# A recurrent attention kernel: one 32-row pass per segment, the left-over rows batched over four segments

## The chip, the cores and the metric

One core of a Trainium2 chip runs the whole kernel. The metric is the device time of one execution in microseconds (us), the median over several runs. A time difference under 2% counts as "the same".

## The reference, cut to what matters

```python
def reference(A_x, A_mem0, A_Wq, A_Wk, A_Wv, A_Wo, A_seg_len, B_x, B_w_r, B_w_gate, B_w_up, B_w_down):
    # x: 1 x 2048 x 1024 bf16; 32 heads of 128; memory M = 8 rows; segments of 32 tokens, so 64 segments
    xn = _layernorm(A_x)
    mem = A_mem0
    for s in range(64):                                  # strictly one after the other, through mem
        h = concat([mem, xn[32*s : 32*s+32]])            # 40 rows
        q, k, v = h @ Wq, h @ Wk, h @ Wv                 # each weight 1024 x 4096
        p = softmax(mask(q @ k.T * scale))               # per head 40 x 40
        o = (p @ v) @ Wo                                 # 4096 x 1024
        mem = o[:8];  outs.append(o[8:])
    # B: the two tokens with the highest router value go through a gated MLP (1024 -> 3584 -> 1024)
    return A_x + concat(outs) + B(xn)
```

The four attention weights are 8 MB each, 32 MB together. Both kernels keep a part of them on chip and stream the rest from HBM (the chip's main memory) again in each of the 64 segments. What comes before the first segment (LayerNorm, the router, the expert MLP of B, the loads of the kept weights) is called the prologue.

## The kernel before

A segment has 40 rows, and the kernel places them on blocks of 32 columns of TensorE's array. So the kernel before makes two passes over every weight: a main pass (PSm: 8 memory rows and 24 token rows) and a left-over pass (PSl: the last 8 token rows, padded to 32). Each group of four matmuls, one per 32-column block of the array, adds one term to a 128x512 result. When a result is complete, ScalarE or VectorE copies it out of TensorE's accumulators; this copy is called its evacuation. The weights are cut into 32 granules (pieces that are loaded as one) of 1 MB; 19 stay on chip and 13 are streamed per segment through four slots (buffers that a granule holds from its issue until TensorE has read it).

```python
N_RES = 19
N_STREAM_BUFS = 4
GCOLS = 4096
# ...
    def get_granule(g):
        if g in res_tiles:
            return granule_view(res_tiles[g], g)
        t = wstream.tile([P, GCOLS], BF16, tag="g")
        nc.sync.dma_start(out=granule_view(t, g), in_=granule_dram(g))
        return granule_view(t, g)
# ...
        for p in range(6):
            mat, half = divmod(p, 2)
            PSm = psA.tile([P, 512], F32, tag="st")
            PSl = psA.tile([P, 512], F32, tag="st")
            for gi in range(KC // 2):
                g = (mat * 2 + half) * (KC // 2) + gi
                Gv = get_granule(g)
                for kk in range(2):
                    kc = 2 * gi + kk
                    for j in range(4):
                        nc.tensor.matmul(PSm[32 * j:32 * j + SEG, :], lhsT=ST[:, kc, :], rhs=Gv[:, kk, 512 * j:512 * (j + 1)],
                                         start=(kc == 0), stop=(kc == KC - 1), tile_position=(0, 32 * j))
                    for j in range(4):
                        nc.tensor.matmul(PSl[32 * j:32 * j + SEG, :], lhsT=STL[:, kc, :], rhs=Gv[:, kk, 512 * j:512 * (j + 1)],
                                         start=(kc == 0), stop=(kc == KC - 1), tile_position=(0, 32 * j))
                for fn in deferred.pop((p, gi), []):
                    fn()
# ... softmax of all heads at once, its tail after the last projection:
            nc.vector.reciprocal(out=DEN[:, 0:NCOL], in_=DEN[:, 0:NCOL])
# ... output projection: two row groups of 32, N = 512
                for dh in range(2):
                    for a in range(2):
                        nc.tensor.matmul(WO[64 * dh + 32 * a:64 * dh + 32 * a + 32, :],
                                         lhsT=OTf[:, NQ * h + 32 * a:NQ * h + 32 * a + 32], rhs=Gv[:, hh, 512 * dh:512 * (dh + 1)],
                                         start=(n_done == 0), stop=(n_done == H - 1), tile_position=(0, 64 * dh + 32 * a))
# ... the small loads and the output stores are issued by GpSimd, the streamed weights by the sync engine:
            nc.gpsimd.dma_start(out=XNR[64 * dh + M:64 * dh + NQ, :], in_=xn_d[t0:t0 + SEG, 512 * dh:512 * (dh + 1)])
```

## Time and profile before

| | before |
|---|---|
| time, median of 4 runs | 3061.8 us (3060.8 to 3063.8) |
| first segment starts at | 210 us |
| one segment | 44.4 us, 64 of them |
| TensorE busy | 82% |
| DMA, mean over the span | 309 GB/s |

These are lines of the page of the kernel before: busy time by engine, and the shares of the chain of work that ended last, by engine and by line.

```profile
...
PE 2510.8 (82%) x44661; PEld 1177.5 (38%) x44725; DVE 1017.0 (33%) x2235; ACT 493.1 (16%) x1013; POOL 344.2 (11%) x782
...
DMA packets 304707, 946.07 MB, mean 309 GB/s; under 512 B 21088, under 2 KB 21104, under 8 KB 304304
...
PE 71%; DVE 17%; DMA 4%; issue 4%; ACT 2%; POOL 1%; another core or an unknown queue 0%; POOLq 0%; DVEq 0%; ACTq 0%
PE PSm L464 20%; PE WO L498 19%; PE PSl L467 18%; PE PTq L377 5%; DVE DEN L425 5%; PE OTP L443 1%; PE OTP L440 1%; DVE MB L169 1%; DVE VM L169 1%; DVE VLs L169 1%; DMA out_dram<-OUTB 1%; ACT MB L169 1%; PE WO L502 1%; DVE NM L395 1%; DVE NMX L405 1%
...
```

The chain says who sets the time: TensorE with 71%, then VectorE (DVE). DMA is only 4% of it. The next lines are the table of time stretches: the whole segment phase, then one segment cut into its stages. The columns are start and end, length, busy time of each engine with its instruction count, the granted TensorE clock, the mean busy share of the 16 DMA engines, and GB/s.

```profile
...
core 0: us, PE busy (x) PEld busy (x) DVE busy (x) ACT busy (x) POOL busy (x), PEclk, DMA share, GB/s
0.00:210.00 210.00, 37.84 (x701) 28.19 (x702) 84.05 (x285) 7.94 (x23) 43.15 (x90) 1.00 0.72 270
210.00:3055.00 2845.00, 2472.98 (x43960) 1149.30 (x44023) 932.92 (x1951) 485.13 (x990) 301.06 (x692) 0.92 0.87 313
1542.79:1568.40 25.61, 25.33 (x469) 11.76 (x470) 9.04 (x22) 4.76 (x11) 1.84 (x4) 1.00 0.97 362
1568.40:1574.68 6.28, 2.89 (x89) 1.75 (x90) 4.36 (x5) 0.59 (x1) 0.26 (x1) 0.84 0.83 312
1574.68:1584.70 10.02, 9.97 (x134) 4.13 (x134) 0.00 (x0) 0.69 (x1) 0.32 (x2) 0.76 0.63 189
1584.70:1587.24 2.54, 0.56 (x8) 0.30 (x5) 1.90 (x6) 0.90 (x2) 2.54 (x6) 1.00 0.88 273
...
```

The third row is the projection stage (25.6 us, TensorE busy for 25.33 of it), then the softmax tail, the output projection at a clock of 0.76, and the handing over of the memory rows. In the projection stage, with a DMA share of 0.97, the weights arrive at 362 GB/s.

### The profile page before, as it was taken

What the parts mean: (1) busy time and instruction counts of PE and PEld (TensorE: products, weight loads), DVE (VectorE), ACT (ScalarE), POOL (GpSimd) and SP (SyncE); (2) the same over time, 40 slices, a digit from 0 to 9 for tenths busy, and PEclk for the clock granted to TensorE, in tenths of its full rate; (3) what the DMA queues carried; (4) which work ended last, traced back from release to release, by engine and by line L of the source; (5) the groups of instructions that cost most, each with busy time, mean ns of one, the idle gap of its engine ahead of it and who ended that gap; (6) DMA issues with size and microseconds to landing.
All of it is one profiled execution on the core that took longest, in us unless ns stands there. A gap on an engine that the chain in (4) does not pass through costs nothing.

```text
span 3059.5 us, 96413 instructions
## 1 busy us (share of the span) xinstructions
PE 2510.8 (82%) x44661; PEld 1177.5 (38%) x44725; DVE 1017.0 (33%) x2235; ACT 493.1 (16%) x1013; POOL 344.2 (11%) x782
## 2 busy tenths in 40 slices
PE   0068888888888888888898888889888888888887
PEld 0043443344444434433443443344344434433443
DVE  5403333332333333333333333333333233333322
ACT  0001111111111111111111111111111111111111
POOL 3201011101101110110011011101101110111010
PEclk9999999999999999999999999999999999999998
DMA  9298898888889888888988898889889888988886
GB/s 378 92 378 302 317 329 303 309 326 308 305 315 330 305 304 319 328 302 308 333 307 299 319 329 303 307 321 321 297 316 333 303 303 315 330 303 309 328 312 220
DMA packets 304707, 946.07 MB, mean 309 GB/s; under 512 B 21088, under 2 KB 21104, under 8 KB 304304
## 3 DMA queue, kind: packets, MB, share of 16 engines
q1 hardware_dynamic: 287904, 914.41, 82.5%
q0 software_dynamic: 16400, 25.49, 2.5%
q8 instruction: 350, 5.73, 0.7%
q14 instruction: 53, 0.43, 0.0%
HBM read 931.42 MB, written 8.40 MB: 307 GB/s over the span
## 4 chain that ended last, share of the span: by engine, by line
PE 71%; DVE 17%; DMA 4%; issue 4%; ACT 2%; POOL 1%; another core or an unknown queue 0%; POOLq 0%; DVEq 0%; ACTq 0%
PE PSm L464 20%; PE WO L498 19%; PE PSl L467 18%; PE PTq L377 5%; DVE DEN L425 5%; PE OTP L443 1%; PE OTP L440 1%; DVE MB L169 1%; DVE VM L169 1%; DVE VLs L169 1%; DMA out_dram<-OUTB 1%; ACT MB L169 1%; PE WO L502 1%; DVE NM L395 1%; DVE NMX L405 1%
## 5 line engine op out<-in xcount | busy, mean ns | idle before, releaser
L464 PE MATMUL PSm<-wres,STn 128*32 128x512 bf16 x7168 | 723.2, 381 | 1.0 <-issue 1.0
L467 PE MATMUL PSl<-wres,STLn 128*32 128x512 bf16 x7168 | 720.0, 379 | 1.3 <-issue 1.3
L464 PE MATMUL PSm<-t,STn 128*32 128x512 bf16 x5120 | 517.1, 382 | 23.9 <-DVE STn L169 13.3
L467 PE MATMUL PSl<-t,STLn 128*32 128x512 bf16 x5120 | 514.1, 379 | 0.0
L464 PEld LDWEIGHTS <-STn 128*32 128x32 bf16 x12288 | 342.0, 96 | 387.7 <-issue 46.7
L467 PEld LDWEIGHTS <-STLn 128*32 128x32 bf16 x12288 | 346.8, 97 | 262.1 <-issue 8.7
L498 PE MATMUL WO<-wres,OTf 128*32 128x512 bf16 x5120 | 399.3, 463 | 0.0
L498 PEld LDWEIGHTS <-OTf 128*32 128x32 bf16 x8192 | 239.5, 114 | 327.5 <-issue 182.9
L440 PE MATMUL OTP<-NMX,VM 32*128 32x40 bf16 x2048 | 96.2, 194 | 198.2 <-DVE NMX L426 144.0
L169 DVE CAST MB<-WO 8x512 bf16<-8x512 f32 x63 | 43.1, 684 | 635.9 <-PE WO L502 330.6
L498 PE MATMUL WO<-t,OTf 128*32 128x512 bf16 x3072 | 252.8, 461 | 0.0
L425 DVE RECIPROCAL DEN<-DEN 128x320 f32<-128x320 f32 x64 | 138.7, 2167 | 170.7 <-PE DEN L424 170.7
L169 DVE CAST XBm<-PSm 128x512 bf16<-128x512 f32 x128 | 88.5, 691 | 307.6 <-PE PSm L464 276.0
L169 DVE CAST XBl<-PSl 128x512 bf16<-128x512 f32 x128 | 88.5, 692 | 232.9 <-PE PSl L467 230.9
L443 PEld LDWEIGHTS <-VLs 32*128 32x128 bf16 x2048 | 78.8, 104 | 205.0 <-issue 205.0
L169 ACT CAST MB<-WO 8x512 bf16<-8x512 f32 x63 | 36.3, 576 | 645.1 <-PE WO L502 328.9
L169 ACT CAST XBm<-PSm 128x512 bf16<-128x512 f32 x128 | 75.0, 586 | 371.5 <-PE PSm L464 349.3
L506 POOL MEMSET MB<- 128x512 bf16 x63 | 33.1, 525 | 851.9 <-PE PTq L377 851.9
L169 ACT CAST XBl<-PSl 128x512 bf16<-128x512 f32 x128 | 75.0, 586 | 292.4 <-PE PSl L467 292.4
L432 POOL MEMSET OTf<- 128x24 bf16 x64 | 7.6, 118 | 876.6 <-PE WO L498 876.1
L377 PE MATMUL PTq<-IDENT,XBm 128*128 128x128 bf16 x1024 | 101.6, 222 | 5.6 <-DVE XBm L169 4.4
L185 PE MATMUL PT<-IDENT,MB 128*128 128x128 bf16 x256 | 24.7, 219 | 97.4 <-ACT STn L169 50.1
(152 smaller groups left out, 2208.9 us busy)
## 6 DMA issues: line engine op xcount, KB each, us to landing
t<-in_A_Wq_dram SPq DMA_DIRECT2D x256, 1024.0 KB, 6.4
t<-in_A_Wk_dram SPq DMA_DIRECT2D x192, 1024.0 KB, 7.7
t<-in_A_Wv_dram SPq DMA_DIRECT2D x192, 1024.0 KB, 8.5
t<-in_A_Wo_dram SPq DMA_DIRECT2D x192, 1024.0 KB, 8.2
Gt<-in_B_w_gate_dram SPq DMA_DIRECT2D x8, 896.0 KB, 12.8
Gt<-in_B_w_up_dram SPq DMA_DIRECT2D x8, 896.0 KB, 8.1
Gt<-in_B_w_down_dram SPq DMA_DIRECT2D x7, 1024.0 KB, 8.0
wres<-in_A_Wk_dram SPq DMA_DIRECT2D x5, 1024.0 KB, 24.4
```

The source lines that it names most:

```text
L169: eng(out=out_ap, in_=in_ap)
L377: nc.tensor.transpose(out=PTq[:, il * P:(il + 1) * P], in_=XBx[:, il * P:(il + 1) * P], identity=IDENT[:, :])
L395: nc.vector.tensor_reduce(out=NM3[:, 0, :], in_=S_main[:, 0:NCOL].rearrange("p (b k) -> p b k", k=32), axis=AX.X, op=ALU.max, apply_transp ...
L405: nc.vector.transpose(out=NMBT, in_=NMX[:, 0:NCOL])
L425: nc.vector.reciprocal(out=DEN[:, 0:NCOL], in_=DEN[:, 0:NCOL])
L440: nc.tensor.matmul(OTP[:, jl, i * NQ:(i + 1) * NQ], lhsT=VM[32 * j:32 * j + SEG, i * P:(i + 1) * P], rhs=P_main[32 * j:32 * j + SEG, i * N ...
L443: nc.tensor.matmul(OTP[:, jl, i * NQ:(i + 1) * NQ], lhsT=VLs[32 * j:32 * j + SEG, i * P:(i + 1) * P], rhs=P_left[32 * j:32 * j + SEG, i * ...
L464: nc.tensor.matmul(PSm[32 * j:32 * j + SEG, :], lhsT=ST[:, kc, :], rhs=Gv[:, kk, 512 * j:512 * (j + 1)], start=(kc == 0), stop=(kc == KC - ...
L467: nc.tensor.matmul(PSl[32 * j:32 * j + SEG, :], lhsT=STL[:, kc, :], rhs=Gv[:, kk, 512 * j:512 * (j + 1)], start=(kc == 0), stop=(kc == KC ...
L498: nc.tensor.matmul(WO[64 * dh + 32 * a:64 * dh + 32 * a + 32, :], lhsT=OTf[:, NQ * h + 32 * a:NQ * h + 32 * a + 32], rhs=Gv[:, hh, 512 * d ...
L502: nc.tensor.matmul(WO[:, :], lhsT=IDENT[:, :], rhs=XR[:, :], start=False, stop=True, skip_group_check=True)
L506: nc.gpsimd.memset(MB[:, :], 0.0)
```

## The change

The intent: take TensorE's work down, and take the stream down with it. The left-over rows of four segments (4 x 8 = 32 rows) make one full pass per four segments; the output projection likewise. The softmax is done by halves of the heads, hidden under projection phases. Half-MB granules let 42 of 64 stay on chip, so 22 x 0.52 = 11.5 MB are streamed per segment in place of 13.6. The price: queries and keys of the left-over rows go through DRAM and come back per segment; the residual, the transposed input rows and the left-over rows' results are further small transfers; and nearly all of them are issued on the weights' own queue.

```diff
-N_RES = 19
-N_STREAM_BUFS = 4
+N_RES = 42
+N_SLOT = 4
+PHASES = [(0, 0), (1, 0), (0, 1), (1, 1), (2, 0), (2, 1)]
... (prologue rewritten: LayerNorm, router and transposes per 128-row tile, results stored to DRAM)
+    def load_st(s):
+        ST = stp.tile([P, KC, SEG], BF16, tag="st", name="ST")
+        nc.sync.dma_start(out=ST.rearrange("p k r -> p (k r)"), in_=xT_d[s // 4][s % 4])
+    def load_stl(g):
+        nc.sync.dma_start(out=STL.rearrange("p k r -> p (k r)"), in_=stl_d[g][:, :])
+    def load_r(s):                       # four loads per segment; load_ql: two loads (QL, KL)
+            nc.sync.dma_start(out=R[32 * g + M:32 * g + SEG, :], in_=xr_d[s * SEG:s * SEG + XM, 256 * g:256 * (g + 1)])
...
+        G, j = divmod(s, 4)
+        if s == 0:
+            left = {0: 0, 1: 0, 2: 0}
+        elif j == 0:
+            left = {2: G}                # V of the left-over rows
+        elif j <= 2 and G + 1 < NT:
+            left = {j - 1: G + 1}        # Q, K of the next four segments' left-over rows
...
+        hook(2, 5, lambda: scores(0))
+        hook(4, 5, lambda: scores(1))
+        hook(5, 2, lambda: attend(0, 0))
+        hook(5, 5, lambda: attend(0, 1))
...
             for kc in range(KC):
+                Gv = granule(8 * p + kc)
+                for jq in range(4):
+                    nc.tensor.matmul(PSm[32 * jq:32 * jq + 32, :], lhsT=ST[:, kc, :], rhs=Gv[:, 512 * jq:512 * (jq + 1)],
+                                     start=(kc == 0), stop=(kc == KC - 1), tile_position=(0, 32 * jq))
+                if PSl is not None:      # only where this segment has a left-over pass
...
         if s + 1 < NSEG:
+            qkl_n = load_ql(s + 1)
+            ST_n = load_st(s + 1)
+            load_r(s + 1)
+            if j == 0 and G + 1 < NT:
+                STL = load_stl(G + 1)
...
+        if j == 3:
+            for g in range(4):
+                for sg in range(4):      # 16 loads of 8 rows
+                    nc.sync.dma_start(out=RL[32 * g + XL * sg:32 * g + XL * (sg + 1), :],
+                                      in_=xr_d[t0:t0 + XL, 256 * g:256 * (g + 1)])
...                                      # and 16 stores of 8 rows from ScalarE's queue (OL)
```

Here j is the segment's place in its group of four. Q and K of the left-over rows of a group are made in the group before it, V and the output in the group itself.

## The prediction

> **What bounds the kernel now.** The table of time stretches, over one segment of 44.45 us (x64 = 2845 us, after a 210 us prologue): 25.6 us of projection passes with TensorE 99% busy; 6.3 us around the softmax tail, where TensorE waits 2.25 us (the reciprocal takes 2.17); 10.0 us of output projection; 2.5 us handing the memory rows to the next segment. So TensorE's chain sets the time (71% of the chain of waits, DMA 4%). In the timeline a group of four 128x512 matmuls advances every 0.216 us; 96 such groups (half for the 8 left-over rows) make 20.7 us, 32 output groups another 6.9. The clock records show 0.5 for 6.8 us in nearly every segment, after the softmax wait; the output groups then take 0.43 us (the Trainium skill, "TensorE: Matmul & The Clock Gate", Part 1, says an idle window halves the clock; the trace agrees). DMA is close behind: 13 one-MB granules per segment; packets of 4096 B take 159 ns and of 2048 B 84 ns on 16 engines (412 and 390 GB/s), so about 33.5 us.
>
> **What changes.** The left-over pass runs once per four segments: 48 + 12 groups, minus 7.8 us. The output projection covers 32 rows, N=256: 3.5 us plus 0.9 on average, minus about 5 us with its half clock. Softmax comes per half, hidden under projections. Hand-over needs one copy, two transposes, one copy: about 1.3 us. I sum TensorE's chain to about 24 us. Streamed weights fall to 22 half-MB granules: 16x1.27 + 6x1.34 = 28.4 us, plus about 1 us of small loads.
>
> **Where the limit goes.** To the weight stream: 29.5 us exceeds 24, so part of TensorE's gain is lost. Nor is the stream continuous. The fastest 1 MB load lands 4.9 us after issue, 2.5 of it data, so fixed latency is about 2.3 us and four half-MB slots (5.1 us of data) leave only about 1 us slack ("DMA: Bandwidth & Descriptors" puts the fixed cost near 2 us). Bubbles I add (estimates): 2 us per segment from hand-over and attention; seven small loads ahead of the output granules at 0.37 us issue each; every fourth segment sixteen 8-row residual loads (about 7 us of queue) that TensorE waits for, then sixteen 8-row stores on ScalarE's queue ahead of the next evacuation (about 6 us). The built program's order shows eight DMA completion semaphores shared by all of these. Estimate: 31.5, 32, 39 and 38 us for the four segments; with half clock in some stalls about 35.5 on average. Prologue: LayerNorm about 4.5 us per tile, expert weights 55 us: about 160 us.
>
> **Predicted: 2430 us** (0.79 of before); 2270 to 2680 eight times in ten. Faster by over 2%: 0.96; within 2%: 0.02; slower: 0.02.
>
> **Right if** DMA is the busiest unit, above 85% in segments at 320 to 340 GB/s; TensorE's matmuls wait mostly for streamed granules; matmuls drop to about 36,000; segments differ with period four, the longest pair around the memory of the fourth; the granted clock stays above 0.8.
>
> **Wrong if** segments are even near 31 us (small transfers free: 2150); or TensorE, about 65% loaded, falls to half clock for most of a segment, when a segment needs 45 us and the gain vanishes; or the attention pieces, now in program order with single buffers, hold TensorE longer than the stream does; or half-size granules stream below 390 GB/s.

## The result, and the profile after

The changed kernel takes 3178.9 us (median of 4 runs, 3167.4 to 3188.6) against 3061.8. The ratio is 1.038, with a 95% interval of 1.0355 to 1.0405: slower, where 0.79 was predicted. (Ratios here are the mean time of one kernel's runs over that of the other's runs of the same rounds, so they are not quite the ratio of the quoted medians.)

| | before | predicted | after |
|---|---|---|---|
| first segment starts at, us | 210 | 160 | 249 |
| mean segment, us | 44.4 | 35.5 | 45.7 |
| segments by j = 0, 1, 2, 3, us | even | 31.5 to 39 | 53.9, 42.0, 41.0, 45.9 |
| matmuls | 44,661 | about 36,000 | 36,305 |
| DMA in the segments | 0.87, 313 GB/s | over 0.85, 320 to 340 | 0.78, 264 |
| granted clock in the segments | 0.92 | above 0.8 (whole run) | 0.82 (whole run 0.836) |

The segments with j = 0 include the very first, which makes three left-over passes; without it their mean is 53.0 us. The two terms of the miss are 249 - 160 = 89 us of prologue and 64 x (45.7 - 35.5) = 653 us of segments.

The page of the changed kernel, the same parts as above (the DMA lines read: packets, MB and mean rate; then packets, MB and share of 16 engines of the weights' queue):

```profile
...
PE 2005.7 (63%) x36305; PEld 1010.8 (32%) x36305; DVE 737.7 (23%) x2158; ACT 447.1 (14%) x1001; POOL 87.9 (3%) x292
...
DMA packets 366682, 831.69 MB, mean 262 GB/s; under 512 B 73428, under 2 KB 118516, under 8 KB 366328
...
q1 hardware_dynamic: 343800, 813.86, 75.8%
...
DMA 57%; PE 25%; DVE 6%; SPq 4%; issue 2%; ACT 2%; ACTq 0%; POOL 0%; DVEq 0%; POOLq 0%
DMA g<-in_A_Wo_dram 16%; DMA g<-in_A_Wq_dram 16%; DMA g<-in_A_Wv_dram 11%; PE PSm L489 10%; DMA g<-in_A_Wk_dram 7%; PE WO L540 6%; PE PSl L493 3%; SPq L532 2%; DMA out_dram<-OB 2%; PE PTq L396 1%; DMA kl_d<-QS 1%; PE WL L540 1%; DMA QL<-ql_d 1%; DVE SPS L438 1%; DVE NM L437 1%
...
```

TensorE's matmuls fell as intended, and its busy time by 505 us (2510.8 to 2005.7). In the segments that is 8.4 us each (38.6 to 30.2, at a granted clock of 0.92 and 0.82), where the prediction's two subtractions, 7.8 and about 5 us, make 12.8. And the chain moved: DMA has 57% of it, TensorE 25%. And yet the busiest DMA queue is at 75.8% only, and all DMA together moves 262 GB/s. So the kernel waits for a stream that isn't running at its rate. The table of stretches of the changed kernel (three of the prologue, the segment phase, and two stretches inside a segment pair):

```profile
...
0.00:144.00 144.00, 35.09 (x384) 26.86 (x384) 60.13 (x245) 35.65 (x49) 38.92 (x36) 1.00 0.62 193
144.00:175.00 31.00, 0.71 (x13) 0.47 (x11) 8.19 (x20) 4.58 (x6) 0.00 (x0) 1.00 0.87 314
175.00:249.00 74.00, 34.18 (x510) 19.79 (x509) 4.32 (x7) 1.03 (x2) 0.00 (x0) 0.94 0.80 276
249.00:3175.00 2926.00, 1935.75 (x35406) 963.65 (x35402) 665.03 (x1887) 405.87 (x945) 48.98 (x256) 0.82 0.78 264
1567.00:1582.20 15.20, 11.41 (x186) 4.76 (x183) 4.68 (x14) 2.37 (x7) 0.38 (x2) 0.78 0.35 125
1582.20:1605.00 22.80, 14.00 (x266) 7.65 (x265) 2.56 (x8) 2.77 (x6) 0.00 (x0) 0.85 0.90 302
...
```

Compare the last two rows. From 1567.0 to 1582.2 us the DMA engines are at 0.35; in the next 22.8 us they are at 0.90 and 302 GB/s. What holds the stream in the first one is seen in the timeline of the sync engine's DMA queue (start, duration of the issue, line, transfer):

```profile
...
1562.90 4.62 SPq L323 DMA_DIRECT2D g<-in_A_Wv_dram  x4
1570.18 0.38 SPq L347 DMA_DIRECT2D QL<-ql_d  x1
1570.61 0.47 SPq L347 DMA_DIRECT2D KL<-kl_d  x1
1571.12 0.47 SPq L328 DMA_DIRECT2D ST<-xT_d  x1
1571.63 1.62 SPq L339 DMA_DIRECT2D RT<-xr_d  x4
1581.76 0.36 SPq L333 DMA_DIRECT2D STL<-stl_d  x1
1582.16 1.97 SPq L323 DMA_DIRECT2D g<-in_A_Wo_dram  x4
```

Between the end of the last Wv granule's issue at 1567.5 and the first Wo granule at 1582.16 no weight is asked for. QL has to wait for its buffer (the queue's own waits, shown below, put 135.5 us over 63 such loads down to the scores that still read it), then KL, ST and four RT follow, and STL waits until 1581.76: its single buffer is being read by the left-over pass of V. All the streamed Wo granules stand behind it in program order, though their four slots are free: four are issued in 1.97 us as soon as STL has gone. The chain then has a 5.2 us piece for the landing of the first Wo granule. In a segment with j = 3 it is the 16 RL loads that stand there (5.3 us of issue), and 11.4 us pass without a granule. These are waits of the sync engine's queue, and one of ScalarE (who waits, line, for what: us in all, times, longest us):

```profile
...
SPq L347 <- PE SPS L432: 135.5, 63, 4.8
...
SPq L333 <- PE PSl L493: 102.1, 15, 8.4
...
SPq L323 <- DMA out_dram<-OB: 73.3, 45, 3.3
...
SPq L323 <- DMA out_dram<-OL: 57.1, 15, 4.6
...
```

```profile
...
ACT XB L500 <- DMA out_dram<-OL: 158.6, 15, 11.6
...
```

The last three lines show a second way in which small transfers hold up the stream, and TensorE as well. In this trace the DMAs of the sync engine and of ScalarE take turns on the same eight completion semaphores (numbers 101 to 108), and each waits until the one before it on its semaphore has landed. So a weight granule (L323) can wait for an output store of ScalarE, 130.4 us in all or 2.0 us per segment, and a store for a granule. The evacuation of the next segment's first result (XB) stands behind such stores in ScalarE's queue, 10.6 us each time after a segment with j = 3.

The waits of TensorE (engine, line, what it waited for: us in all, times, longest us):

```profile
...
PE WO L540 <- DMA g<-in_A_Wo_dram: 242.9, 181, 5.0
PE PSm L489 <- DMA g<-in_A_Wq_dram: 176.1, 175, 3.6
PE PTq L396 <- ACT XB L500: 161.8, 78, 9.7
PE PSm L489 <- DMA g<-in_A_Wv_dram: 110.1, 114, 3.0
...
PE PSm L489 <- DMA g<-in_A_Wk_dram: 72.6, 83, 2.5
PE WL L534 <- DMA RL<-xr_d: 61.8, 16, 5.0
```

Added up over all gaps between instructions, TensorE stands 15.4 us per segment, of which 9.4 us end with a streamed granule's landing. The rest is in its own chain: transposes (PTq) that wait for ScalarE's evacuation of a projection (XB), the RL loads (residual rows for the left-over output), and VL (the evacuated values of the left-over rows).

### The profile page after: what moved, and what is told of

The parts are those of the page before. It is cut to its first block, busy times and chain, and to the rows that moved or that the text cites. A ratio compares the mean times of both kernels' runs of the same rounds, so it can differ in the third digit from the quotient of the medians.

```text
span 3180.1 us, 81705 instructions
## 1 busy us (share of the span) xinstructions
PE 2005.7 (63%) x36305; PEld 1010.8 (32%) x36305; DVE 737.7 (23%) x2158; ACT 447.1 (14%) x1001; POOL 87.9 (3%) x292
## 3 DMA queue, kind: packets, MB, share of 16 engines
q1 hardware_dynamic: 343800, 813.86, 75.8%
## 4 chain that ended last, share of the span: by engine, by line
DMA 57%; PE 25%; DVE 6%; SPq 4%; issue 2%; ACT 2%; ACTq 0%; POOL 0%; DVEq 0%; POOLq 0%
DMA g<-in_A_Wo_dram 16%; DMA g<-in_A_Wq_dram 16%; DMA g<-in_A_Wv_dram 11%; PE PSm L489 10%; DMA g<-in_A_Wk_dram 7%; PE WO L540 6%; PE PSl L493 3%; SPq L532 2%; DMA out_dram<-OB 2%; PE PTq L396 1%; DMA kl_d<-QS 1%; PE WL L540 1%; DMA QL<-ql_d 1%; DVE SPS L438 1%; DVE NM L437 1%
## 5 line engine op out<-in xcount | busy, mean ns | idle before, releaser
L489 PE MATMUL PSm<-wres,ST 128*32 128x512 bf16 x8192 | 789.7, 428 | 15.5 <-DVE ST L356 14.3
L489 PE MATMUL PSm<-g,ST 128*32 128x512 bf16 x4096 | 451.7, 428 | 362.8 <-DMA g<-in_A_Wq_dram 176.1
L489 PEld LDWEIGHTS <-ST 128*32 128x32 bf16 x12288 | 330.5, 101 | 815.5 <-issue 499.8
L540 PEld LDWEIGHTS <-OT 128*32 128x32 bf16 x8192 | 260.4, 117 | 335.4 <-issue 286.0
L540 PE MATMUL WO<-g,OT 128*32 128x256 bf16 x3072 | 203.9, 354 | 243.8 <-DMA g<-in_A_Wo_dram 242.9
L540 PE MATMUL WO<-wres,OT 128*32 128x256 bf16 x5120 | 302.6, 350 | 0.0
L500 ACT CAST XB<-PSm 128x512 bf16<-128x512 f32 x256 | 149.5, 584 | 784.0 <-PE PSm L489 477.3
L493 PE MATMUL PSl<-wres,STL 128*32 128x512 bf16 x2048 | 221.7, 418 | 49.6 <-DVE VL L513 48.3
L396 PE MATMUL PTq<-IDENT,XB 128*128 128x128 bf16 x1024 | 112.0, 238 | 163.9 <-ACT XB L500 161.8
L493 PE MATMUL PSl<-g,STL 128*32 128x512 bf16 x1024 | 112.5, 423 | 6.1 <-DVE XBl L504 6.1
```

The lines of the kernel that those rows point to most:

```text
L396: nc.tensor.transpose(out=PTq[:, il, :, :].rearrange("p j r -> p (j r)"), in_=XB[:, il * P:(il + 1) * P], identity=IDENT[:, :])
L489: nc.tensor.matmul(PSm[32 * jq:32 * jq + 32, :], lhsT=ST[:, kc, :], rhs=Gv[:, 512 * jq:512 * (jq + 1)], start=(kc == 0), stop=(kc == KC - ...
L493: nc.tensor.matmul(PSl[32 * jq:32 * jq + 32, :], lhsT=STL[:, kc, :], rhs=Gv[:, 512 * jq:512 * (jq + 1)], start=(kc == 0), stop=(kc == KC - 1),
L500: nc.scalar.copy(out=XB[:, :], in_=PSm[:, :])
L540: nc.tensor.matmul(PS[32 * g:32 * g + 32, 0:256], lhsT=lhs(h), rhs=Gv[:, D * hs + 256 * g:D * hs + 256 * (g + 1)], start=False, stop=(last ...
```

## The experiments

The theories, in the letters of this text:

- **Q, queue**: small transfers on the weights' queue, and what each of them waits for, stop the stream.
- **D, depth**: four half-MB slots hold about 5 us of stream, as long as a granule takes from issue to landing, so every pause of TensorE is also a pause of the stream.
- **C, chain**: TensorE's own chain is far longer than the 24 us of the prediction.
- **K, clock**: TensorE waits so much that it runs at half clock, and that makes the segments long.

The expectations have letters of their own. In them theory A is depth (D here), B a stream bound by its bytes, C the small transfers (Q here), rival D of e_nostream TensorE's own chain or its clock (C and K here), E the queue order inside that chain, and F the clock. Those of e_slots5 use Q and D as here.

All fourteen kernels were judged correct against the reference. Three of them compute something wrong on purpose (they are marked). They still pass, presumably because the attention output is small beside the residual, which no run tested; the check of correctness is blind to this fault, and says nothing for them. The experiments ran on four chips, and beside them the kernel before had its median between 3060.3 and 3061.2 us. Times are medians of several runs; segment times come from the one profiled execution of each kernel.

### Depth at the cost of bytes: e_slots8

```diff
-N_RES = 42
-N_SLOT = 4
+N_RES = 38
+N_SLOT = 8
```

> The changed kernel with 38 granules kept and 8 stream slots in place of 42 and 4: 26 granules streamed per segment in place of 22, the same memory. Theory A (four half-MB slots are too few: issue to landing takes about 5 us, so the ring is bound by latency): the expert-weight part of the prologue, where TensorE is never the limit, falls from 68 us to about 55, and segments fall from 45.7 to about 41 us, total about 2880. Rival B (the stream is bound by bytes): segments grow by 26/22, to 50 us or more, total 3400 or more.

Measured: 3249.7 us, ratio 1.062 [1.0605, 1.0642]. The segments grew to 47.0 us on average, though the longest (j = 0) shrank from 53.9 to 52.5. The first segment started 17.5 us earlier. It matches neither figure. Eight slots cost four more granules per segment, so two effects are mixed here; e_depth22 below separates them.

### Fewer small transfers: e_merge

The 16 RL loads become 4, the 16 OL stores become 4, with the same bytes.

```diff
-                for sg in range(4):
-                    t0 = (4 * G + sg) * SEG + XM
-                    nc.sync.dma_start(out=RL[32 * g + XL * sg:32 * g + XL * (sg + 1), :],
-                                      in_=xr_d[t0:t0 + XL, 256 * g:256 * (g + 1)])
+                nc.sync.dma_start(out=RL[32 * g:32 * g + 32, :],
+                                  in_=xr_d[P * G:P * (G + 1), 256 * g:256 * (g + 1)].rearrange(
+                                      "(s r) c -> s r c", r=SEG)[:, XM:SEG, :])
... (the OL stores alike)
```

> The changed kernel with the sixteen 8-row residual loads and the sixteen 8-row stores of every fourth segment merged into four each; nothing else. Theory C (the gaps in the stream come from small transfers queued in front of it): the fourth segment falls from 45.9 to about 41 us and the one after it from 53.9 to about 49, total about 3040. Theory A (slots alone): within 1% of the changed kernel, 3150 to 3190.

Measured: 3032.4 us, ratio 0.992 [0.9903, 0.994]. Segments 43.5 us: those with j = 0 went from 53.9 to 48.3 and those with j = 3 from 45.9 to 43.2; the other two moved by 0.6 us or less. So 24 of the transfers per four segments cost 2.2 us per segment on average, at unchanged bytes. The total is close to what theory C of the expectation gave (3040), though j = 3 fell to 43.2 us and not to 41. Little of the gain shows as less waiting for weights, however. TensorE's waits for streamed granules fell only from 9.4 to 8.8 us per segment. What fell are its waits for XB (161.8 to 77.2 us in all), as ScalarE's wait behind the OL stores fell from 158.6 to 59.4 us, and its waits for RL (61.8 to 15.3 us).

### The small loads off the weights' queue: e_poolq

On top of e_merge, the loads of QL, KL, ST, STL, RT and RL are issued by GpSimd.

```diff
-        nc.sync.dma_start(out=ST.rearrange("p k r -> p (k r)"), in_=xT_d[s // 4][s % 4])
+        nc.gpsimd.dma_start(out=ST.rearrange("p k r -> p (k r)"), in_=xT_d[s // 4][s % 4])
... (STL, RT, QL, KL, RL alike)
```

> As the merged one, and all small loads of a segment (left-over queries and keys, token columns, residual rows) issued from GpSimd's queue, so that the queue of the weight stream holds weights only, as in the kernel before. Theory C: the gaps before the output granules (5 to 14 us without an issue) go, segments fall to about 37 us, total about 2620. Theory A: the stream is still 22 granules at about 1.45 us or more, so no segment falls below 36, and the unmerged 42 us segments fall little; total about 2850 to 2950.

Measured: 2895.9 us, ratio 0.9475 [0.9437, 0.9513]. Segments 41.3 us (44.7, 39.9, 37.7, 43.0). Another 2.2 us per segment; together with e_merge it turns the change from a loss of 4% into a gain of 5%. TensorE's waits for granules fell from 8.8 to 6.9 us per segment. Small transfers as a whole thus have 4.4 us of the 10.2 us per segment, but how much of them belongs to theory Q in the strict sense, the weights' queue, stays open, since e_merge's half shows mostly in TensorE's own chain. The 2620 us of the expectation's theory C were missed by 276 us; the total lies in the range given for depth (2850 to 2950), and no group of segments has a mean below 36 us. One thing isn't separated here: in the traces the DMAs of GpSimd have eight completion semaphores of their own (112 to 119), so the move took away the small loads' issue (3.9 us of the sync engine's queue per segment in e_merge), their waits for buffers, and their use of the weights' semaphores at once.

### No stream at all (wrong): e_nostream

Each streamed granule is replaced by a kept one, so the arithmetic is the same in amount and wrong in value.

```diff
-        if g in res_tiles:
-            return res_tiles[g]
+        while g not in res_tiles:
+            g -= 1 if g else -2
+        return res_tiles[g]
```

> Wrong results on purpose: every streamed granule of the segments is replaced by a kept one, so no weight is streamed after the prologue; all else as the changed kernel. If the stream is what sets the time (theories A to C), segments fall to about 28 us (my sum of TensorE's chain was 24, plus waits for small transfers) and the clock rises to above 0.95: total about 2050. Rival D (the attention pieces in program order, or the half clock, hold TensorE): segments stay above 38 us, total above 2650.

Measured: 2385.3 us, ratio 0.779 [0.7775, 0.7801]. Segments 33.4 us (38.2, 31.5, 29.8, 34.2). This is TensorE's chain with nothing to wait for but the kernel's own small work, and it is 33.4 us, not 24: 26.2 us of busy TensorE and 7.1 us of waits. It lies between the two expectations (28, and above 38). Taking the stream away saves 45.7 - 33.4 = 12.3 us, but theory C holds too. Of the 12.3 us, 8.3 are waits (15.4 to 7.1), and 4.0 are busy time (30.2 to 26.2): the same matmuls ran at a granted clock of 0.90 in place of 0.82. The waits of this run, in the form as above:

```profile
...
PE PTq L397 <- ACT XB L501: 151.7, 147, 5.7
...
PE OP L469 <- DVE VM L511: 89.4, 48, 1.9
PE WL L535 <- DMA RL<-xr_d: 58.6, 15, 4.9
...
```

Three pieces of chain show: a transpose waits for ScalarE (XB), which sits in its queue behind DMA issues, the QS buffer and the second softmax's exponential; an attention piece waits for VectorE's half of the V evacuation (VM), which stands behind the second softmax; and the left-over projection waits for RL.

### The chain relieved, no stream (wrong): e_nostream_chain

On top of e_nostream: DMA issues moved from ScalarE to GpSimd, QS in its own buffer, the V evacuation on ScalarE alone, the second softmax two granules earlier and the first attention pieces two later.

```diff
-            QS = two.tile([P, 4, 16, XL], BF16, tag="xb", name="QS")
+            QS = two.tile([P, 4, 16, XL], BF16, tag="qs", name="QS", bufs=1)
-            nc.scalar.dma_start(out=dst.rearrange("p s c -> p (s c)"), in_=QS.rearrange("p s h r -> p (s h r)"))
+            nc.gpsimd.dma_start(out=dst.rearrange("p s c -> p (s c)"), in_=QS.rearrange("p s h r -> p (s h r)"))
-        hook(4, 5, lambda: scores(1))
-        hook(5, 2, lambda: attend(0, 0))
-        hook(5, 5, lambda: attend(0, 1))
+        hook(4, 3, lambda: scores(1))
+        hook(5, 4, lambda: attend(0, 0))
+        hook(5, 7, lambda: attend(0, 1))
-                nc.scalar.copy(out=VM[:, c0:c0 + 256], in_=PSm[:, 0:256])
-                nc.vector.tensor_copy(out=VM[:, c0 + 256:c0 + 512], in_=PSm[:, 256:512])
+                nc.scalar.copy(out=VM[:, c0:c0 + 512], in_=PSm[:, :])
... (VL and the other stores alike)
```

> Wrong results on purpose: no weight streamed, as in the earlier run, and TensorE's own chain relieved: stores issued from GpSimd in place of ScalarE, own buffer for the left-over transposes, value evacuations all on ScalarE, second softmax two granules earlier, first attention two granules later. Theory E (the chain without a stream is 33 us because evacuations stand behind softmax steps and stores in the in-order queues): it falls by 3 us per segment or more, total 2200 or less. Rival: it is TensorE's own work at a lower clock, and stays above 2330.

Measured: 2262.2 us, ratio 0.739 [0.7379, 0.7403]. Segments 31.3 us. The queue order of ScalarE and VectorE was worth 2.2 us, less than the 3 that theory E asked for, and the total lies between the two expectations. Some 31 us is the floor of the changed kernel's TensorE chain as these edits leave it: 25.4 us busy, 5.8 us of waits.

### Depth at equal bytes (wrong): e_depth22

Eight slots and 38 kept granules, as in e_slots8, but four of the 26 streamed granules are replaced by kept ones, so that 22 are streamed as before.

```diff
+    keep22 = set(g for i, g in enumerate(sorted(streamed)) if i not in (3, 9, 16, 22))
...
+        while g not in res_tiles and g not in keep22:
+            g -= 1 if g else -2
```

> Wrong results on purpose: 8 stream slots in place of 4, and the same 22 granules per segment streamed (the four extra streamed ones of the 8-slot kernel are replaced by kept ones). It tells the depth of the ring apart from its bytes. If four slots are too few (theory A), it is well below the changed kernel: a segment of about 41 us, total about 2850. If depth is worth little, within 2% of the changed kernel.

Measured: 2981.7 us, ratio 0.973 [0.9712, 0.9748]. Segments 43.0 us, and the first one starts at 232 us. So depth by itself is worth 2.7 us per segment and 16 us of prologue in the changed kernel. That is 6% of its time, between the two expectations: more than the 2% that would have made depth worth little, and not the 41 us of theory A. Beside e_slots8 (47.0 us), the four extra granules cost 4.0 us, 1.0 us each.

### Keeping the clock up: e_warm

Two matmuls with zero weights before each streamed granule, adding nothing to the sums.

```diff
+                if kc > 0 and 8 * p + kc in streamed:
+                    for _ in range(2):
+                        nc.tensor.matmul(PSm[:, :], lhsT=ZW[:, :], rhs=res_tiles[0][:, 0:512], start=False, stop=False,
+                                         skip_group_check=True)
... (alike before the streamed Wo granules)
```

> The changed kernel with two matmuls of a zero matrix ahead of each streamed granule (sums unchanged), which TensorE does while it would wait; 7.5 us of extra TensorE work per segment at full clock. Theory F (half clock after waits costs several us per segment): the mean granted clock rises from 0.84 to above 0.93 and the time falls to about 3050. Rival (half clock is only a sign of waiting): the clock rises and the time stays or grows, 3180 or more.

Measured: 3262.4 us, ratio 1.066 [1.0635, 1.0678]; segments 47.0 us. The clock rose from 0.836 to 0.92, as in the kernel before, and the kernel got slower. The added matmuls have a price of their own (TensorE is busy for 2467 us, 461 more), so this doesn't show that the low clock costs nothing; the 4.0 us of busy time in e_nostream say that it may cost up to that. It shows that a clock like before's, bought this way, doesn't bring the time back. In the later runs the clock rises by itself as waits are taken away, to 0.934.

### The levers together: e_best

e_poolq, the chain's relief of e_nostream_chain, RL loaded one segment earlier, and the LayerNorm loop turned round so that a tile's transposes come a step later.

> The kernel with small loads on GpSimd's queue and merged, plus the relief of TensorE's chain, the residual rows loaded a segment earlier, and LayerNorm tiles overlapped one stage more in the prologue. The terms added: prologue 245 to about 195 us; segments 41.3 to about 38 us; total about 2640. If only the stream's rate counts (22 granules at about 1.6 us), segments stay above 40 and the total above 2780.

Measured: 2770.0 us (6 runs, 2751 to 2782), ratio 0.907 [0.9058, 0.9088]. Segments 38.8 us, with the period of four nearly gone (38.5, 39.8, 39.0, 38.0). It beats both kernels but misses its own expectation by 130 us. 60 us of that is the prologue: the first segment starts at 255 us, 6 us later than in the changed kernel, not at about 195. The rest is in the segments, where TensorE still waits 7.5 us for granules.

### Why the turned loop won nothing: e_ln_dve

In e_best's prologue, these are groups of instructions (line, engine, operation, result and source, shapes, count; busy us and mean ns of one; idle time before and what ended it):

```profile
...
L195 POOL TENSOR_TENSOR DX<-XT,XN 128x1024 bf16<-128x1024 bf16 x11 | 23.3, 2115 | 80.6 <-ACT XN L183 80.6
L158 DVE CAST mvrb<-mv 128x2 bf16<-128x2 f32 x11 | 21.2, 1930 | 0.4
...
```

A cast of 128x2 numbers takes 1.93 us, in every tile just while GpSimd's residual add of 2.1 us runs. In the changed kernel the two don't meet and the same cast takes 0.17 us. "Trainium Architecture — The Big Picture", section "What this means for kernel authors", in the Trainium skill says that VectorE and GpSimd share a port pair under an exclusive lock. The test moves the add to VectorE:

```diff
-        nc.gpsimd.tensor_tensor(out=DX[:, :], in0=XT.pop(t)[:, :], in1=XN[:, :], op=ALU.add)
+        nc.vector.tensor_tensor(out=DX[:, :], in0=XT.pop(t)[:, :], in1=XN[:, :], op=ALU.add)
```

> Question: why did turning round the LayerNorm loop in the combined version win nothing in the prologue (first segment at 255 us, 249 with the change as given)? In the combined version's trace a DVE cast of 128x2 takes 1.93 us in each tile, whenever GpSimd's residual add (2.12 us) runs; in the changed kernel, where the two don't meet, the same cast takes 0.17 us. This run is the combined version with only that add moved from GpSimd to DVE. Theory L1 (the DVE stands still while GpSimd adds): the 128x2 cast falls to about 0.17 us, the add costs DVE about 0.6 us, and the first segment starts 15 to 30 us earlier, at 225 to 240 us; total 2740 to 2755 against 2770. Rival L2 (the loop is bound by something else, such as the store of the residual tile that the DVE's subtraction waits for, up to 2.8 us per tile): the cast gets short but the first segment moves by less than 10 us; total 2760 to 2775.

Measured: 2767.5 us (e_best 2770.0), first segment at 258 us.

```profile
...
L195 DVE TENSOR_TENSOR DX<-XT,XN 128x1024 bf16<-128x1024 bf16 x7 | 4.8, 691 | 8.9 <-ACT XN L183 8.9
...
L158 DVE CAST mvrb<-mv 128x2 bf16<-128x2 f32 x7 | 1.2, 172 | 0.2
...
```

The cast fell to 172 ns, so the blocking was real and this trace agrees with the skill. But it was not what bounds the loop: rival L2 held. These are the waits of the same run over the same stretch, in which seven tiles pass:

```profile
...
PE PR L209 <- ACT XTS L205: 51.1, 7, 8.4
...
ACT XN L183 <- DVE DX L182: 29.7, 7, 5.4
ACT sd L175 <- DVE verf L160: 22.6, 7, 3.2
...
DVE RROW L214 <- PE PR L211: 8.2, 8, 1.0
```

The loop is a ring of in-order queues. The router's matmuls wait for XTS, which stands on ScalarE's queue behind the square root of the next tile, which waits for VectorE, whose queue waits for the casts of the router's result.

### The loop in an order without the ring: e_ln_order

```diff
     for t in range(NT + 3):
         if t >= 3:
             ln_d(t - 3)
+        if 2 <= t <= NT + 1:
+            ln_c(t - 2)          # transposes, evacuation, router matmuls
+            ln_d2(t - 2)         # store of the residual
         if 1 <= t <= NT:
             ln_b(t - 1)          # scaling
...
             ln_a(t)              # statistics
+        if 1 <= t <= NT:
+            ln_b2(t - 1)         # residual add, on VectorE
         if 2 <= t <= NT + 1:
-            ln_c(t - 2)
+            ln_c2(t - 2)         # casts of the router's result
```

> The combined version with the LayerNorm loop put in an order in which no in-order engine waits for the same tile's chain: transposes and evacuation of tile t-2 first, then the scaling of t-1, the statistics of t, the residual add of t-1 on DVE, and last the two router casts of t-2; the residual store is issued one step earlier. DVE's own work is then about 5 us per tile. Theory L3 (my prediction's 4.5 us per tile was wrong because each in-order engine has to sit through the chain DVE, ACT, PE, ACT, DVE of a single tile): tiles fall from 8.5 us to 5 to 6.5, first segment at 190 to 210 us, total 2705 to 2730. Rival L4 (the loop is bound by the weight and input transfers that share its queue): tiles stay above 7.5 us, first segment above 230, total above 2745.

Measured: 2712.2 us, ratio 0.887 [0.8842, 0.8892]. The first segment starts at 197 us, a tile takes about 5.8 us (12 tiles in 70 us) in place of 8.8, and the segments are unchanged at 38.9 us. Theory L3 held in all its numbers.

### One slot more: e_ln_order5

```diff
-N_RES = 42
-N_SLOT = 4
+N_RES = 41
+N_SLOT = 5
```

> The same with 41 granules kept and 5 slots, 23 streamed, in the same memory. Depth theory: with the small transfers off the weights' queue there is still about 7.6 us of TensorE waiting for granules per segment and the stream moves about 0.52 MB per 1.5 us; one more slot hides more of each landing than one more granule costs: segments 37 to 38.5 us against 38.8, total 20 to 110 us below the run with 4 slots, and the expert weights some 5 us faster. Rival (the stream is at the rate it can have, about 340 GB/s when busy, and depth no longer counts): one more granule costs 1.5 us, segments 40 or more, total 60 to 100 us above.

Measured: 2559.6 us, ratio 0.837 [0.8355, 0.8388]; segments 36.7 us, first one at 189 us. The depth theory held, and by more than it claimed: 153 us for one slot, although one more granule has to be streamed.

### How far depth goes: e_ln_order6 and e_ln_order8

The same with 40 kept granules and 6 slots, and with 38 and 8.

> 40 kept, 6 slots, 24 streamed, all else as the version with 5 slots (2560 us, segments 36.7 us, mean DMA share 0.98 at 348 GB/s). Saturation theory: at a DMA share of 0.98 the stream has no idle time left that more depth could fill, so one more granule of 0.52 MB costs its 1.5 us: segments 37.7 to 38.5, total 2615 to 2680. Depth theory (the granule's landing is still exposed, as it was with 4): segments 36 or less, total 2440 to 2540.

> 38 kept, 8 slots, 26 streamed, all else as the version with 5 slots. Saturation theory: 26 granules and about 0.5 MB of small transfers at 348 GB/s take 41 us: segments 40.5 to 42, total 2800 to 2900. Depth theory: below 39 us, total below 2700.

Measured: 2470.4 us (2463.4 to 2472.3), ratio 0.8065 [0.8051, 0.8079], segments 35.6 us, with 6 slots; 2555.9 us, ratio 0.835 [0.8335, 0.8365], segments 37.0 us, with 8. The saturation theory, which I took from the DMA share of 0.98, was wrong both times. One row each of the table of stretches, from 400 to 2400 us, for the changed kernel and then for the relieved version with 4, 5, 6 and 8 slots (the last three columns are clock, DMA share and GB/s):

```profile
...
400.00:2400.00 2000.00, 1326.30 (x24193) 659.69 (x24186) 456.36 (x1294) 277.12 (x646) 33.79 (x176) 0.82 0.79 264
...
```

```profile
...
400.00:2400.00 2000.00, 1467.48 (x28806) 747.02 (x28806) 493.73 (x1408) 355.50 (x770) 458.08 (x953) 0.91 0.92 315
...
```

```profile
...
400.00:2400.00 2000.00, 1538.03 (x30485) 787.66 (x30481) 520.26 (x1487) 373.57 (x812) 482.50 (x1007) 0.90 0.98 347
...
```

```profile
...
400.00:2400.00 2000.00, 1552.86 (x31363) 804.61 (x31352) 536.81 (x1536) 385.07 (x837) 495.47 (x1035) 0.93 1.01 374
...
```

```profile
...
400.00:2400.00 2000.00, 1527.62 (x30275) 780.05 (x30271) 518.95 (x1482) 371.69 (x808) 479.56 (x998) 0.92 1.03 389
...
```

The rate goes on rising, 315, 347, 374, 389 GB/s, after the share has reached 0.98. A share of this kind counts how long packets were under way, not what the engines could carry: it passes 1. What changes with depth is in the records of the packets of 4096 bytes on the weights' queue: their median is 159 or 160 ns in all these runs, but their mean falls from 189 to 180, 170 and 166 ns, as the slow few become fewer. With 8 slots the stream is fastest, but it has two granules more to carry than with 6.

### Depth alone in the changed kernel: e_slots5

The changed kernel with 41 kept granules and 5 slots, nothing else.

> The changed kernel as given (3179 us, segments 45.7 us, DMA share 0.78 at 263 GB/s), only with 41 kept and 5 slots, 23 streamed. Theory Q (in the changed kernel the small transfers of the same queue stop the stream for 12 to 15 us at a time, longer than any depth of half-MB slots covers; a fifth slot helps between those stops only): segments 44.5 to 46, total 3090 to 3190. Rival D (depth alone was the fault; it is worth the same 2.2 us per segment here as in the version with the small transfers moved): segments 43.5 or less, total 3040 or less.

Measured: 3072.2 us, ratio 1.002 [0.9985, 1.0062] of the kernel before; segments 44.4 us (53.0, 40.0, 39.3, 45.4), first one at 238 us. It lies between the two expectations. The slot brings 1.3 us per segment here (1.5 by the medians, since the profiled execution was the slowest of four) and 2.2 in the relieved version, and mostly in the segments with j = 1 and 2 (2.0 and 1.6 us); those with j = 0 and 3, in which the queue stops, hardly move (0.9 and 0.5 us). So depth and small transfers are two faults, and the second hides part of what the first is worth. The shared semaphores may have a part in that: with the fifth slot the granules' waits for output stores rise from 130.4 to 219.8 us, and in the relieved version, whose stores go through GpSimd, there are none. No run gives the stores semaphores of their own and changes nothing else, so what they cost stays open.

## Why the prediction was wrong

It was right on the work: matmuls (36,305), the period of four with the longest segments around j = 3 and the one after it, TensorE's waits being mostly for streamed granules, and the clock just above 0.8. It named depth, small transfers, the store queue of ScalarE, the eight shared semaphores and the rate of half-MB granules as risks. Its sign that DMA would be above 85% busy at 320 to 340 GB/s did not come (0.78 and 264). It went wrong in the sum.

| term, as predicted | measured |
|---|---|
| prologue about 160 us, LayerNorm about 4.5 us per tile | 249 us; a tile takes 8.8 us in a ring of in-order queues (e_ln_order: 5.8 us, first segment at 197); the expert weights took 74 us at 276 GB/s, not 55 |
| TensorE's chain about 24 us | 33.4 us without any stream (e_nostream): 26.2 busy, 7.1 waiting; 31.3 with better queue order |
| stream 28.4 + 1 us, at 412 and 390 GB/s | 315 GB/s with four slots and a free queue, 389 with eight |
| bubbles, 6 us on average | small transfers 4.4 us (e_merge, e_poolq); depth 2.7 us at equal bytes (e_depth22) |
| the limit is the longer of chain and stream | chain 33.4 us; stream alone about 33 us (estimate: 12.06 MB per segment, from 264 GB/s times 45.7 us, at the 362 GB/s of before's projection stage); together 45.7 us |

**The step that failed first** is "To the weight stream: 29.5 us exceeds 24", with a sum of bubbles on top. Both numbers were too small, and the two don't overlap as that step supposes. The chain was in the main a sum of matmul times, and as such nearly right: without the stream TensorE is busy 26.2 us, 12.4 less than before, where 12.8 were forecast. It left out that the projections wait for evacuations that stand in ScalarE's and VectorE's queues, 7.1 us in all with the RL loads. Slower matmuls under a lower clock (30.2 us busy in the changed kernel, at 0.82) were in it only as part of the last step, to 35.5 us. The stream was computed from the median packet. The mean in the kernel before was 182 ns, and its own projection stage shows 362 GB/s at a share of 0.97; reading that row instead of the packet would have given 33 us. With a chain of 33 and a stream of 33 there is no slack on either side, so a stop of one can be added to the other. This last step is argued and not shown: no run measured the stream alone. With six slots and the chain relieved, a segment takes 35.6 us beside a chain of about 31 and a DMA share of 1.01; there the longer of the two all but sets the time.

**Where the expected gain went** can be followed from version to version: 45.7 us per segment; 43.5 with the small transfers merged; 41.3 with them off the weights' queue; 38.8 with the chain relieved; 36.7 with a fifth slot; 35.6 with a sixth. The prologue goes from 249 to 255, 197, 189 and 184 us. The last version takes 2470 us. That this lies inside the range predicted for the change itself is no confirmation, since it is another kernel. But the idea of the change was sound. What took the gain was the small transfers on the queues (and perhaps the semaphores) of the weights and of ScalarE, the number of slots, and the order of work on the evacuating engines.

The steps of this ladder were each taken on top of the ones before. e_slots5 shows that their sizes depend on that order, so they are not a unique split of the 10.1 us.

**The clock** follows the waits, and is probably in part a cause: the same matmuls keep TensorE busy for 30.2 us per segment at 0.82 and for 26.2 at 0.90 (e_nostream). e_warm raised it to 0.92 at no gain, but at a price of its own. What a higher clock at no price would bring stays open. Open too is why a few packets take far longer than the median when fewer granules are in flight, and what the 5.8 us of waits in the floor of 31 us would take to remove.

## What to carry to other kernels

Before halving the bytes or the work of a stage, put its chain and its stream side by side as the trace has them (the mean rate of a stretch in which the stream is never stopped, and the time between dependent stages with their evacuations), and if they come out alike, expect more than the longer of the two as long as the slots are few. Keep small loads that wait for a buffer off the in-order queue of a weight stream, look which completion semaphores the stream shares with other transfers, and count the slots in granules' landing times: with smaller granules more of them are needed, and here giving up two kept granules for two more slots was worth 240 us of 2712. A DMA share near 1 doesn't prove that the stream is at its limit; try one more slot and look at the rate.

## What the Trainium skill lacked or had wrong

- "DMA: Bandwidth & Descriptors", section "Issuing engines are not separate DMA queues", says that issuing from several engines saves only the sequencer's time for issuing, usually small. Here moving six kinds of small loads from the sync engine to GpSimd saved 2.2 us per segment (e_merge 3032.4, e_poolq 2895.9 us), which isn't small. Their issue alone takes 3.9 us of the sync engine's queue per segment in e_merge, so the saving could be issue time, as the page has it. In an in-order queue a small load also brings the wait for its buffer ahead of the weights (14.6 us without a granule in the timeline shown, 3.3 of them issue), of which the page says nothing here. The move changed the completion semaphores too, and no run separates the three. The nearest advice is in "Perfetto Trace Analysis", section "DMA Optimizations", which suggests one engine for inputs and one for outputs.
- The same page, section "Bandwidth", gives the rate by size of one transfer, issued from GpSimd (1 MB: 341 GB/s, and the rule to batch to 1 MiB or more). It has nothing on the number in flight. Granules of 0.52 MB ran at 315, 347, 374 and 389 GB/s with 4, 5, 6 and 8 slots.
- "Perfetto Trace Analysis" has no number that shows how far the DMA busy share of a profile can mislead. Here the share stood at 0.98 at 347 GB/s and 1.03 at 389 GB/s.
- "TensorE: Matmul & The Clock Gate", Part 1, tells how idling lowers the clock, and the trace of before agrees in that (0.76 in the output projection after the softmax wait). The page gives the idle window as about 3.4 us; here the clock fell to 0.5 after a wait of 2.25 us, the longest gap that TensorE's records show in any segment of before. The page doesn't warn that raising it with filler matmuls can cost more than it brings: clock 0.836 to 0.92, time 3179 to 3262 us.
- "Trainium Architecture — The Big Picture" is right on the port lock of VectorE and GpSimd (cast 1930 ns against 172 ns). Taking the block away changed the time by nothing measurable here (2770.0 to 2767.5 us).
